# A planned attention and MLP block: prologue over four PSUM banks with keys first, another form of the normalization, an own home for the last group's outputs, contiguous value bursts

## The chip, the cores and the metric

The kernel runs on one core of a Trainium2 chip. The metric is the device time in microseconds (us) of one execution; a kernel's time is the median of its runs. Profiles are taken by the hardware profiler on one execution. The engines are PE (matmuls; PEld is its weight load), DVE (vector), ACT (scalar, with exponential and tanh), POOL (GpSimd) and SP, which issues the DMAs.

## The reference

```
x = A_x                                    # 1 x 2048 x 1024, bf16
xn = layernorm(x)
qkv = xn @ wqkv                            # 32 heads of 32
p = softmax(q k^T * 32**-0.5)
s = (p v, heads joined) @ wo
y = layernorm(xn)                          # the MLP normalizes again
h = gelu(y @ w1 + b1)                      # tanh form, 1024 -> 3584
g = silu(h @ w2 + b2)                      # 3584 -> 1024
out = x + s * g
```

## The kernel before

All work is first written down as a list of operations, each with the tiles it reads and writes, an assumed duration and a priority. A planner (`_Plan.run`) then plays the five engines forward in time with these assumed durations and so fixes the order of instructions on each engine; `settle` derives the semaphore waits from it. On the chip each engine goes through its list in that order and stops where a wait is not yet fulfilled, whatever stands behind it.

**The opening ("pro").** The 2048 tokens are sixteen tiles of 128. For a pair of tiles DVE takes the statistics (L657, L659), POOL raises variance + epsilon to the power -0.5 (L664) and normalizes each tile (L667: subtract the mean, then multiply by the reciprocal deviation) into one of four buffers `xnb`. PE transposes the tile into a PSUM bank (L644), and ACT copies it to `xnT` (L647; the profile names it `big`). From two transposed tiles PE makes queries and keys of the first head group together (one bank, L634 takes both out to `qk`), and values (L617).

**The second normalization.** Its scale per token comes from the first one's variance: four small POOL operations (L679 to L683), the last a power over all sixteen tiles, then a store to DRAM (L684) and a load that spreads 256 tokens' scales over all partitions (`sbc`, L715). Between the two SP also issues the loads of the biases b1 (L685) and b2 (L686). DVE multiplies `xnT` by `sbc` to make `yT` (L718), the MLP's input for 256 tokens.

**Attention.** The 32 heads form eight groups of four. A unit is one group, 256 queries and 256 keys; there are 512. For a unit PE makes scores into four of six PSUM banks (0 to 5; L862), ACT takes two exponentials of 128x1024 into one of nine buffers `P` (L871), DVE adds the two key blocks (`PA`, L874), and PE multiplies with the values and, from `PA` and a tile of ones, the sums of the softmax. Eight units make a group of queries: their value products go into one bank as a burst ("pv"), and DVE divides by the sums (L901 to L907). A burst is opened, in the planner, after the exponential of the sixth unit of its group (`xs[5]`). Outputs of the first seven head groups are stored to DRAM (L950) and reloaded for the last projection (L924); those of the eighth are written straight into `OTr`, which lies where `xnT` was, once nobody reads `xnT` any more (the list `dead`).

**Dense work.** Projections of the next head group ("proj"), the MLP ("mlp": w1, GELU in L738 to L748, w2, L775 to L780) and the output projection ("wo") run in items that fill one PSUM bank each. Together with the value bursts they have banks 6 and 7. All these matmuls are issued by the helper `quad`, so they share the line L544; the tiles' names tell them apart.

In the planner PE takes scores first, then the open burst, then dense chunks, with a pace that holds scores back where dense work lags. The opening's items are taken strictly in the order of their list.

Of the kernel before, what the change touches and what calls it, by code (L numbers as in the profile page):

```python
# [30 lines left out]
class _Plan:  # L31
# [46 lines left out]
    def run(self, total_units, dense_slack):  # L78
# [9 lines left out]
        bank_free = {6: [], 7: []}  # L88
        owner = {6: None, 7: None}
        heads = {q: 0 for q in self.queues}  # L90
        dense_total = sum(c.occ for q in ("proj", "mlp", "wo") for it in self.queues[q] for c in it.chunks)
# [13 lines left out]
        def commit(o, t):  # L105
            e = o.eng
            o.start = t
            if e == "SP":
                tf[e] = t + o.occ
                state["bw"] = max(state["bw"], t) + o.nbytes / 170.0  # L110
                o.fin = state["bw"] + 1900.0
            else:
                tf[e] = t + o.occ
                o.fin = t + o.occ + o.lat
            order[e].append(o)
            self.seq.append(o)
            release(o, t)
            wake(tf[e], e)
# [66 lines left out]
        def pe_step(t):  # L185
            cands = []
            nxt = INF
            if state["s"] < len(self.s_queue):
                o = self.s_queue[state["s"]]
                if o.left == 0:  # L190
                    cands.append((o.ready, 0, o, None))
# [25 lines left out]
            else:  # L217
                bf = bank_for(t)
                if bf is not None:
                    for n in next_items(t):  # L220
                        it = self.queues[n][heads[n]]
# [169 lines left out]
def bass_recurrent_scan__mha_block__mixer_channel_mlp__prompt_kernel(  # L391
# [14 lines left out]
    HG = 8  # L406
# [17 lines left out]
    plan = _Plan()  # L424
    add = plan.add

    with ExitStack() as st:
# [22 lines left out]
        wv = qk0[:, 4096 + 3072:4096 + 3072 + 2048].rearrange("p (c n) -> p c n", c=DC)  # L450
        wo_sb = qk0[:, 0:8192].rearrange("p (c n) -> p c n", c=HG)
# [23 lines left out]
        lnp = sb("lnp", [128, NT, 4], F32)  # L475
# [19 lines left out]
        def c_ps(n):  # L495
            return 133 + 1.04 * n
# [103 lines left out]
        def v_item(pr, n, kind, due=0):  # L600
# [20 lines left out]
        def qk_pair_item(n):  # L621
            it = _Item("pro")
            for k in range(8):
                w, dcs = k // 4, (2 * (k % 4), 2 * (k % 4) + 1)
# [9 lines left out]
            dve(lambda e: e.tensor_copy(QKT[0][:, :, n * 256:(n + 1) * 256],  # L634
                                        bank(it.bank).rearrange("p (w s) -> p w s", w=2)),
                c_ps(512), [], [("Q", 0, n), ("K", 0, n)], 0, it)
# [17 lines left out]
        for n in range(NPR):  # L654
            for t in (2 * n, 2 * n + 1):
                for c in range(2):
# [6 lines left out]
                [("mv", lo), ("mv", lo + 1)], [("ve", n)], 1)  # L663
            pool(lambda e, lo=lo, hi=hi: e.tensor_tensor(lnp[:, lo:hi, 1], lnp[:, lo:hi, 0], mhalf[:, lo:hi], op=ALU.pow),  # L664
                 450, [("ve", n), ("mhalf",)], [("rs", n)], 0)
            for t in (lo, lo + 1):
                pool(lambda e, t=t: e.tensor_scalar(xnb[t % 4], xst[t], mv[:, t, 0:1], lnp[:, t, 1:2],  # L667
                                                    op0=ALU.subtract, op1=ALU.mult), 950,
                     [XS(t), ("mv", t), ("rs", n)], [("xnb", t % 4)], 1)
            its = [tr_item(lo), tr_item(lo + 1), qk_pair_item(n), v_item(0, n, "pro")]  # L670
            if n == 0:
                pro_q += its[0:3]
                late = its[3]
            else:
                pro_q += its[0:3] + [late]
                late = its[3]
        pro_q.append(late)
# [174 lines left out]
        def unit(u, pv):  # L852
# [3 lines left out]
            b0 = [(4 * u + j) % 6 for j in range(4)]  # L856
# [53 lines left out]
        OTr = xnT  # L910
        for w in range(HG):
            if w + 1 < HG:
                proj(w + 1, w)
            else:

                dead = []
                for t in range(NT):
                    for d in [plan.last_w[("xnT", t)]] + plan.readers[("xnT", t)]:
                        if d not in dead:
                            dead.append(d)  # L920
                wdead = [("Q", 0, n) for n in range(NPR)] + [("K", 0, n) for n in range(NPR)] + \
                        [("wqk", i) for i in range(3)] + [("wv",)]
                for hg in range(HG - 1):
                    dma(f"otl{hg}", lambda e, hg=hg: e.dma_start(OTr[:, hg, :], o_d[hg]), 524288,  # L924
                        [("o_d", hg, q) for q in range(NQB)], [("OTr", hg)], extra=dead)
                dma("wo", lambda e: e.dma_start(wo_sb, A_wo.rearrange("(c p) n -> p c n", p=128)), 2097152, [],
                    wdead + [("wo",)])
            for qb in range(NQB):
# [16 lines left out]
                pv.trigger = xs[5] if g < HG * NQB - 1 else xs[0]  # L945
# [7 lines left out]
                norm(g, pv, OTr[:, w, qb * 256:(qb + 1) * 256], [("OTr", w, qb)], dead)  # L953

                for t2 in range(2):
# [18 lines left out]
                    for nh in range(2):  # L974
                        it = _Item("wo")
                        for hc in range(HG):
                            def fn(e, b, hc=hc, tb=tb, nh=nh):
                                return quad(e, lambda j: bankp(b, j, 0, 512),
                                            lambda j: OTr[:, hc, tb * 128 + 32 * j:tb * 128 + 32 * j + 32],
# [72 lines left out]
```

## Time and profile before

| | |
|---|---|
| median of 2 runs | 1227.2 us (1226.93 to 1227.46) |
| profiled execution | 1225.87 us, span 1224.1 us |
| busy, PE / ACT / DVE / POOL | 1069.9 / 1040.2 / 848.6 / 71.2 us |
| exponentials (1024) | 976.5 us of ACT, 1111 ns each |
| HBM traffic | 143.40 MB read, 12.07 MB written |

The profile names a line by L and its number, then the tile written and the tiles read. An engine's idle time is put down to what ended it. PE instructions are pipelined, so a burst's duration divided by its count, not the mean of one, is what a matmul costs.

### The profile page before, as it was taken

The page shows a single profiled execution, that of the slowest core. Times are in us where ns is not written, and L with a number is a line of the kernel's source. Part 1 is how long each engine was busy: PE and PEld are TensorE (multiplying, and loading weights), DVE is VectorE, ACT ScalarE, POOL GpSimd, SP SyncE. Part 2 cuts the span into 40 slices and gives each one's busy share as a digit, 9 for nine tenths or more (in the row PEclk, how much of TensorE's full clock was granted, in tenths as well). Part 3 has the DMA queues.
Part 4 walks back from the last instruction along what each step waited for, and adds up shares of the span by engine and source line. Part 5 has one row for each costly group of instructions (what it writes and reads, how often), then busy time and mean ns, then how long its engine had stood idle before and what let it go on. Part 6 is the DMA issues. An engine that isn't in the chain of part 4 may idle for free.

```text
span 1224.1 us, 63652 instructions
## 1 busy us (share of the span) xinstructions
PE 1069.9 (87%) x30080; PEld 717.9 (59%) x30080; DVE 848.6 (69%) x1531; ACT 1040.2 (85%) x1186; POOL 71.2 (6%) x34
## 2 busy tenths in 40 slices
PE   4636999999999999999999998999989997778998
PEld 2524666756766576656776566656766664456443
DVE  4613897778676886786668866976678776554676
ACT  2414998999899999998999988999999999866894
POOL 6960000000000000000000000000000000000000
PEclk8876999999999999999999999999999998789999
DMA  7032446633365445533365445533355456426242
GB/s 232 2 61 52 121 128 179 179 99 85 109 172 156 137 142 159 162 85 102 108 183 147 126 126 167 169 97 90 103 168 147 134 149 210 142 75 193 83 141 96
DMA packets 289268, 159.55 MB, mean 130 GB/s; under 512 B 28912, under 2 KB 278768, under 8 KB 289008
## 3 DMA queue, kind: packets, MB, share of 16 engines
q1 hardware_dynamic: 289008, 155.49, 44.4%
q8 instruction: 235, 3.85, 1.3%
q14 instruction: 25, 0.20, 0.1%
HBM read 143.40 MB, written 12.07 MB: 127 GB/s over the span
## 4 chain that ended last, share of the span: by engine, by line
PE 49%; ACT 37%; POOL 5%; DVE 5%; issue 3%; SPq 1%; DMA 1%; POOLq 0%; ACTq 0%; DVEq 0%
PE ps L544 41%; ACT P L871 34%; PE ps L862 8%; POOL gw L667 4%; ACT ut L746 2%; SPq L686 1%; DVE PA L874 1%; ACT gw L779 1%; DVE nt L901 1%; DMA sbc<-s_scratch 1%; DVE xb L738 0%; POOL lnp L664 0%; PE ps L644 0%; DVE V L617 0%; DVE ut L744 0%
## 5 line engine op out<-in xcount | busy, mean ns | idle before, releaser
L871 ACT ACTIVATE P<-ps 128x1024 bf16<-128x1024 f32 x1024 | 976.5, 1111 | 136.6 <-PE ps L862 135.9
L874 DVE TENSOR_TENSOR PA<-P 128x1024 bf16<-128x1024 bf16 x512 | 351.7, 688 | 210.1 <-ACT P L871 204.3
L544 PE MATMUL ps<-yT,w1r 128*32 128x256 bf16 x7168 | 238.6, 273 | 12.7 <-DVE QKT L831 3.9
L544 PE MATMUL ps<-w2r,hT 128*32 128x256 bf16 x7168 | 232.3, 273 | 12.0 <-issue 5.2
L544 PEld LDWEIGHTS ps<-yT,w1r 128*32 128x32 bf16 x7168 | 178.5, 96 | 55.4 <-issue 29.5
L544 PEld LDWEIGHTS ps<-w2r,hT 128*32 128x32 bf16 x7168 | 182.4, 97 | 41.7 <-issue 27.4
L544 PE MATMUL ps<-P,V 128*32 128x256 bf16 x4096 | 170.7, 280 | 16.8 <-issue 8.6
L544 PE MATMUL ps<-big,qk 128*32 128x512 bf16 (+1 forms) x2304 | 141.5, 374 | 14.5 <-ACT big L647 8.5
L544 PE MATMUL ps<-qk,big 128*32 128x256 bf16 (+1 forms) x3072 | 137.1, 318 | 6.7 <-DVE gw L775 1.4
L862 PE MATMUL ps<-qk 32*128 32x256 bf16 x2048 | 104.7, 277 | 40.6 <-DVE qk L634 25.2
L544 PEld LDWEIGHTS ps<-P,V 128*32 128x32 bf16 x4096 | 104.9, 98 | 45.1 <-ACT P L871 18.1
L544 PE MATMUL ps<-PA,ones 128*32 128x256 bf16 x2048 | 126.4, 277 | 1.9 <-issue 1.6
L862 PE MATMUL ps<-QKT 32*128 32x256 bf16 x2048 | 103.5, 276 | 23.0 <-ACT P L871 22.1
L544 PEld LDWEIGHTS ps<-qk,big 128*32 128x32 bf16 x3072 | 77.8, 99 | 46.3 <-issue 13.1
L544 PEld LDWEIGHTS ps<-big,qk 128*32 128x32 bf16 x2304 | 57.5, 102 | 63.3 <-issue 15.1
L862 PEld LDWEIGHTS ps<-qk 32*128 32x128 bf16 x2048 | 30.9, 92 | 107.5 <-ACT P L871 65.7
L746 ACT ACTIVATE ut<-ut 128x512 f32<-128x512 f32 x112 | 83.4, 745 | 4.3 <-DVE ut L744 4.1
L738 DVE TENSOR_TENSOR xb<-ps,b1T 128x512 bf16<-128x512 f32 x112 | 76.8, 686 | 14.2 <-PE ps L544 13.7
L748 DVE SCALAR_TENSOR_TENSOR hT<-ut,xb 128x512 bf16<-128x512 f32 x112 | 76.1, 680 | 15.1 <-ACT ut L746 14.7
L862 PEld LDWEIGHTS ps<-QKT 32*128 32x128 bf16 x2048 | 30.7, 92 | 94.4 <-ACT P L871 80.8
L744 DVE SCALAR_TENSOR_TENSOR ut<-sq,xb 128x512 f32<-128x512 bf16 x112 | 76.7, 684 | 1.0
L544 PEld LDWEIGHTS ps<-PA,ones 128*32 128x32 bf16 x2048 | 57.3, 98 | 22.7 <-issue 13.7
(45 smaller groups left out, 466.3 us busy)
## 6 DMA issues: line engine op xcount, KB each, us to landing
w1r<-in_B_w_dram SPq DMA_DIRECT2D x112, 512.0 KB, 4.2
w2r<-in_B_w_dram SPq DMA_DIRECT2D x128, 448.0 KB, 4.4
qk<-in_A_wqkv_dram SPq DMA_DIRECT2D x16, 256.0 KB, 3.1
g_scratch<-gw SPq DMA_DIRECT2D x32, 128.0 KB, 2.9
o_scratch<-ot SPq DMA_DIRECT2D x56, 64.0 KB, 2.8
big<-o_scratch SPq DMA_DIRECT2D x7, 512.0 KB, 6.5
hT<-in_A_x_dram SPq DMA_DIRECT2D x10, 256.0 KB, 7.4
qk<-in_A_wqkv_dram SPq DMA_DIRECT2D x4, 512.0 KB, 4.4
```

The source lines that it names most:

```text
L544: ins = e.matmul(dst(j), lhsT=lhsT(j), rhs=rhs(j), start=start, stop=stop, tile_position=(0, 32 * j), skip_group_check=True)
L667: pool(lambda e, t=t: e.tensor_scalar(xnb[t % 4], xst[t], mv[:, t, 0:1], lnp[:, t, 1:2], op0=ALU.subtract, op1=ALU.mult), 950, [XS(t), ("m ...
L686: dma("b2", lambda e: e.dma_start(b2b[:], B_b2.rearrange("(o d) -> o d", o=1).to_broadcast([128, D])), 262144, [("s3",)], [("b2",)])
L738: dve(lambda e: e.tensor_tensor(xb_t[i3][:].rearrange("p (k t) -> p k t", k=2), bank(it.bank).rearrange("p (k t) -> p k t", k=2), b1T[:, 2 ...
L744: dve(lambda e: e.scalar_tensor_tensor(ut_t[i3][:], sq_t[p % 2][:], 1.0 / GA, xb_t[i3][:], op0=ALU.add, op1=ALU.mult), c_f32(512), [("sq", ...
L746: act(lambda e: e.activation(ut_t[i3][:], ut_t[i3][:], ACT.Tanh, scale=GC * GA), c_act(512), [("ut", i3)], [("ut", i3)], 1)
L748: dve(lambda e: e.scalar_tensor_tensor(hT[:, hs].rearrange("p k t -> p (k t)"), ut_t[i3][:], 1.0, xb_t[i3][:], op0=ALU.add, op1=ALU.mult), ...
L779: act(lambda e: e.activation(zh_t[zi], z_t[zi], ACT.Tanh, scale=0.5), c_act(512), [("z", zi)], [("zh", zi)], 1)
L862: ins = e.matmul(bank(b0[j], kk * 256, (kk + 1) * 256), lhsT=QKT[sl][32 * j:32 * j + 32, 1, kb * 128:(kb + 1) * 128], rhs=QKT[sl][32 * j:3 ...
L871: x = act(lambda e, h=h: e.activation(P[pi][:, 2 * h:2 * h + 2].rearrange("p j k q -> p (j k q)"), ps[:, pr[h] * 1024:(pr[h] + 1) * 1024], ...
L874: pa = dve(lambda e: e.tensor_tensor(PA[ai][:], P[pi][:, :, 0, :], P[pi][:, :, 1, :], op=ALU.add), c_b16(1024), [("P", pi, 0), ("P", pi, 1 ...
L901: a = dve(lambda e: e.transpose(nt_t[i][:], bank(pv.bank, 256, 512)), c_ps(256), [], [("nt", i)], 1, pv)
```

## The change

It has five parts.

1. **Prologue banks and order.** While the opening's transposes, keys and first queries are under way ("due" 0), its items may also use PSUM banks 4 and 5 (`flex`); the first eight units of scores (`NARROW`) stay in banks 0 to 3, and the ninth waits until 4 and 5 are free. Keys are made for every pair of tiles, but queries only for the first two pairs' tokens: those of pair 0 with its keys, those of pair 1 as an item of its own. Queries of the other tokens become three 512-wide items of "proj". Values follow two pairs behind. Of the next eight opening items the planner now takes one that is ready.
2. **Normalization.** POOL now multiplies by the reciprocal deviation and adds a bias, `x * r + (-mean * r)`. The negated mean is one more small DVE operation a pair, its product with r one more small POOL operation a pair.
3. **Last group's outputs** go into `ot7`, a piece of `qk0` behind `wo_sb`, and wait only for the readers of the value weights that lay there.
4. **Value bursts** open after the eighth exponential (`TRIG` = 7).
5. **The planner's assumptions**: DVE's reads of PSUM shorter by 63 ns, DMA at 210 in place of 170 bytes a nanosecond, the small power at 700 in place of 450 ns, and DVE does not begin an operation of low priority shortly before one of high priority falls due.

```
-        bank_free = {6: [], 7: []}
+        bank_free = {b: [] for b in (4, 5, 6, 7)}
+        flex = [6, 7, 4, 5]
...
-                state["bw"] = max(state["bw"], t) + o.nbytes / 170.0
+                state["bw"] = max(state["bw"], t) + o.nbytes / 210.0
...
+            if best is not None and e == "DVE" and best.prio >= 2 and soon[e]:
+                r = min((x[0] for x in soon[e] if x[2].prio <= 1), default=INF)
+                if r < t + best.occ - 400:
+                    wake(r, e)
+                    return None
...
-            for b in (6, 7):
+            for b in flex:
...
+                if state["s"] == self.narrow:
+                    if len(flex) == 2 and o.left == 0 and all(owner[b] is None or owner[b].k == len(owner[b].chunks) for b in (4, 5)):
...
+                        if n == "pro":
+                            q = self.queues["pro"]
+                            best = None
+                            for k in range(heads["pro"], min(len(q), heads["pro"] + 8)):
...
+                            if best[1].due == 0:
+                                state["early"] -= 1
+                                if state["early"] == 0:
+                                    del flex[2:]
+                            q.insert(heads["pro"], q.pop(k))
...
+        ot7 = qk0[:, 8192:10240]
...
-            return 133 + 1.04 * n
+            return 70 + 1.04 * n
...
+        def k_pair_item(n, with_q):
+            return pair_item(n, (1, 0) if with_q else (1,))
+        def q_pair_item(n):
+            return pair_item(n, (0,))
...
+            dve(lambda e, lo=lo, hi=hi: e.tensor_scalar_mul(lnp[:, lo:hi, 4], mv[:, lo:hi, 0], -1.0), 65,
+                [("mv", lo), ("mv", lo + 1)], [("nm", n)], 1)
...
+            pool(lambda e, lo=lo, hi=hi: e.tensor_tensor(lnp[:, lo:hi, 5], lnp[:, lo:hi, 4], lnp[:, lo:hi, 1], op=ALU.mult),
+                 200, [("nm", n), ("rs", n)], [("nb_", n)], 0)
             for t in (lo, lo + 1):
-                pool(lambda e, t=t: e.tensor_scalar(xnb[t % 4], xst[t], mv[:, t, 0:1], lnp[:, t, 1:2],
-                                                    op0=ALU.subtract, op1=ALU.mult), 950,
+                pool(lambda e, t=t: e.tensor_scalar(xnb[t % 4], xst[t], lnp[:, t, 1:2], lnp[:, t, 5:6],
+                                                    op0=ALU.mult, op1=ALU.add), 950,
...
+            pro_q += [tr_item(lo), tr_item(lo + 1), k_pair_item(n, n == 0)]
+            if n >= 2:
+                pro_q.append(v_item(0, n - 2, "pro"))
+        pro_q.append(q_pair_item(1))
+        pro_q.append(v_item(0, 6, "pro"))
+        pro_q.append(v_item(0, 7, "pro"))
...
-            b0 = [(4 * u + j) % 6 for j in range(4)]
+            k0 = 0 if u < NARROW else 2 * (u - NARROW) + 2
+            b0 = [(2 * k0 + j) % 6 for j in range(4)]
...
+        for tq in range(1, 4):
+            plan.queues["proj"].append(qk_item(0, 0, tq, wq0, 16 * tq - 12))
...
-                pv.trigger = xs[5] if g < HG * NQB - 1 else xs[0]
+                pv.trigger = xs[TRIG] if g < HG * NQB - 1 else xs[0]
...
-                norm(g, pv, OTr[:, w, qb * 256:(qb + 1) * 256], [("OTr", w, qb)], dead)
+                norm(g, pv, ot7[:, qb * 256:(qb + 1) * 256], [("OTr", w, qb)], dead7)
```

Some lines of the last output projection follow from `ot7` and are not shown.

More of the change, by code (lines that the diff above doesn't have):

```diff
@@ L87, in run @@
                  "done": 0.0, "last_bank": 7}
-        bank_free = {6: [], 7: []}
-        owner = {6: None, 7: None}
+        bank_free = {b: [] for b in (4, 5, 6, 7)}
+        owner = {b: None for b in (4, 5, 6, 7)}
+        flex = [6, 7, 4, 5]
         heads = {q: 0 for q in self.queues}
+        state["early"] = sum(it.due == 0 for it in self.queues["pro"])
         dense_total = sum(c.occ for q in ("proj", "mlp", "wo") for it in self.queues[q] for c in it.chunks)
@@ L189, in pe_step @@
                 o = self.s_queue[state["s"]]
-                if o.left == 0:
+                if state["s"] == self.narrow:
+                    if len(flex) == 2 and o.left == 0 and all(owner[b] is None or owner[b].k == len(owner[b].chunks) for b in (4, 5)):
+                        xs = bank_free[4] + bank_free[5]
+                        if all(x.start is not None for x in xs):
+                            cands.append((max([o.ready] + [x.fin for x in xs]), 0, o, None))
+                            for x in xs:
+                                o.deps[x] = True
+                elif o.left == 0:
                     cands.append((o.ready, 0, o, None))
@@ L920, in bass_recurrent_scan__mha_block__mixer_channel_mlp__prompt_kernel @@
                             dead.append(d)
-                wdead = [("Q", 0, n) for n in range(NPR)] + [("K", 0, n) for n in range(NPR)] + \
+                wdead_ = [("Q", 0, n) for n in range(NPR)] + [("K", 0, n) for n in range(NPR)] + \
                         [("wqk", i) for i in range(3)] + [("wv",)]
+                dead7 = [d for d in [plan.last_w[("wv",)]] + plan.readers[("wv",)]]
                 for hg in range(HG - 1):
```

48 lines of the change are left out of this document (29 added, 19 removed).

## The prediction

> **What bounds it now.** I read the page first, then busy time by stretches, then the opening in order of time, then the waits. The page gives the span, each engine's share, and the span in 40 slices of 30.6 us.
>
> ```profile
> span 1224.1 us, 63652 instructions
> PE 1069.9 (87%) x30080; PEld 717.9 (59%) x30080; DVE 848.6 (69%) x1531; ACT 1040.2 (85%) x1186; POOL 71.2 (6%) x34
> PE   4636999999999999999999998999989997778998
> POOL 6960000000000000000000000000000000000000
> ```
>
> PE and ACT are both near full for most of the run, so neither alone is the bound. Two stretches fall short: the first four slices, the only ones in which POOL works, and slices 33 to 36. The stretches show it (columns: window, length, then busy us of PE, PEld, DVE, ACT, POOL, granted clock, DMA share, GB/s):
>
> ```profile
> 72.00:80.00 8.00, 1.31 (x48) 1.01 (x40) 0.00 (x0) 0.00 (x0) 8.00 (x3) 0.87 0.17 12
> 80.00:90.00 10.00, 0.00 (x0) 0.00 (x0) 0.00 (x0) 0.00 (x0) 1.95 (x1) 0.50 0.40 34
> 400.00:500.00 100.00, 93.45 (x2748) 63.76 (x2748) 77.60 (x141) 97.39 (x113) 0.00 (x0) 1.00 0.53 148
> 1000.00:1050.00 50.00, 38.44 (x1032) 24.50 (x1028) 31.68 (x55) 45.44 (x53) 0.00 (x0) 0.86 0.56 171
> 1050.00:1100.00 50.00, 36.01 (x924) 23.72 (x920) 29.24 (x53) 36.16 (x41) 0.00 (x0) 0.83 0.36 113
> ```
>
> The opening in order of time (start, length, engine, line, tiles; in brackets the idle time before and what ended it):
>
> ```profile
> 36.45 7.54 POOL L667 TENSOR_SCALAR gw<-hT,mv,lnp 128x1024 bf16<-128x1024 bf16 x2
> 44.78 7.54 POOL L667 TENSOR_SCALAR gw<-hT,mv,lnp 128x1024 bf16<-128x1024 bf16 x2
> 71.47 2.94 POOL L683 TENSOR_TENSOR lnp<-lnp,mhalf 128x16 f32<-128x16 f32 x1
> 74.40 7.55 POOL L667 TENSOR_SCALAR gw<-w2r,mv,lnp 128x1024 bf16<-128x1024 bf16 x2
> 74.44 0.37 SPq L684 DMA_DIRECT2D s_scratch<-lnp  x1
> 75.84 11.06 SPq L686 DMA_DIRECT2D b2b<-in_B_b_dram  x1
> 88.02 9.81 SPq L715 DMA_DIRECT2D sbc<-s_scratch  x2
> 94.37 1.90 DVE L718 TENSOR_TENSOR yT<-big,sbc 128x512 bf16<-128x512 bf16 x3 [24.57 <-DMA sbc<-s_scratch]
> 96.92 0.61 PE L862 MATMUL ps<-qk 32*128 32x256 bf16 x8 [23.62 <-DVE qk L634]
> 97.47 3.60 PE L544 MATMUL ps<-qk,big 128*32 128x256 bf16 x64
> 124.05 0.62 PE L544 MATMUL ps<-yT,w1r 128*32 128x256 bf16 x16 [0.77 <-DVE QKT L831]
> ```
>
> Up to 82 us the opening goes at POOL's pace, 8.33 us a pair of tiles. Then the second norm's scale goes through DRAM: its power ends at 74.41, DVE gets it at 94.37, and what is queued behind DVE's wait keeps PE still for 23.6 us. The MLP starts at 124.05. From there on both engines are near full (93.45 and 97.39 of 100), so what is saved before it moves the end by as much.
>
> **The normalization's price.** One tile costs 7.54 / 2 = 3.77 us. Rows for bounds:
>
> ```profile
> 0.24 0.10 POOL L1037 MEMSET const-float32-0.0<- 128x1 f32 x1 [0.24 <-issue]
> 0.82 0.24 POOL L587 IOTA iota_i<- 128x128 int32 x1 [0.39 <-POOLq L1037]
> 6.65 0.71 POOL L664 TENSOR_TENSOR lnp<-lnp,mhalf 128x2 f32<-128x2 f32 x1 [5.05 <-DVE lnp L662]
> 70.45 0.24 POOL L679 TENSOR_TENSOR lnp<-mv,lnp 128x16 f32<-128x16 f32 x1
> 71.09 0.30 POOL L682 TENSOR_SCALAR lnp<-lnp 128x16 f32<-128x16 f32 x1
> ```
>
> High end: 3.77, the same tile in the old form. Low end: the IOTA writes 127 elements a partition more than the MEMSET in 0.14 us, 1.1 ns each; 1024 of them and 0.10 make 1.2 us. The old form's 3.7 ns an element is no limit of moving data, and not contention: from 74.40 it takes 7.55 a pair while DVE is idle. On POOL the operation sets the price: the power takes (2.94 - 0.71) / 14 = 0.16 us an element, while 16 multiplies or 16 adds fit in 0.24 to 0.30. The new form multiplies, then adds. I take 1.2, with 3.77 as the first rival.
>
> The Trainium skill (GPSIMD Engine Reference, Engine selection) has one-input operations on this engine at about line rate; at its 1.2 GHz that is an estimate of 0.9 us, and the sum would be 1 us lower. The old form at 3.77 does not agree, so the page cannot tell the two forms apart. Its Key points speak against the change: POOL shares an interface with VectorE. By that the faster form could slow down beside DVE's statistics; the 7.54 and 7.55 with DVE busy and idle show none of it for the old form.
>
> **The opening, step by step.** On POOL the second scale now stands last:
>
> ```order
> L713 TENSOR_TENSOR lnp<-lnp,mhalf 128x2
> L718 TENSOR_SCALAR gw<-w2r,lnp 128x1024
> L715 TENSOR_TENSOR lnp<-lnp 128x2
> L728 TENSOR_TENSOR lnp<-mv,lnp 128x16
> L718 TENSOR_SCALAR gw<-w2r,lnp 128x1024 x2
> L730 TENSOR_TENSOR lnp<-lnp 128x16
> L731 TENSOR_SCALAR lnp<-lnp 128x16
> L732 TENSOR_TENSOR lnp<-lnp,mhalf 128x16
> ```
>
> Before, the power (L683) stood ahead of the last two tiles. On DVE, where yT waits for that scale, before:
>
> ```order
> L874 TENSOR_TENSOR PA<-P 128x1024
> L718 TENSOR_TENSOR yT<-big,sbc 128x512 x3
> L634 CAST qk<-ps 128x2x256
> L718 TENSOR_TENSOR yT<-big,sbc 128x512
> L617 CAST V<-ps 128x2x2x128
> ```
>
> and now:
>
> ```order
> L653 CAST V<-ps 128x2x2x128
> L924 TENSOR_TENSOR PA<-P 128x1024
> L682 CAST qk<-ps 128x256
> L767 TENSOR_TENSOR yT<-big,sbc 128x512 x3
> L653 CAST V<-ps 128x2x2x128
> L767 TENSOR_TENSOR yT<-big,sbc 128x512
> L924 TENSOR_TENSOR PA<-P 128x1024 x2
> L653 CAST V<-ps 128x2x2x128
> ```
>
> All keys are now out of PSUM ahead of yT; two value casts and the first group's value product are left behind it (before, also the last two transposes and the last two key pairs). So PE still stops for sbc, but less waits behind it. Prices for DVE and PE:
>
> ```profile
> 10.67 0.61 DVE L662 TENSOR_SCALAR lnp<-mv 128x2 f32<-128x2 f32 x1
> 17.22 3.24 PE L544 MATMUL ps<-big,qk 128*32 128x256 bf16 x64 [1.11 <-ACT big L647]
> 20.52 0.69 DVE L634 CAST qk<-ps 128x512 bf16<-128x512 f32 x1 [9.24 <-PE ps L544]
> 22.44 0.21 DVE L659 BATCH_NORM_AGGREGATE mv<-stats 128x2 f32<-128x12 f32 x1
> 23.83 0.21 DVE L659 BATCH_NORM_AGGREGATE mv<-stats 128x2 f32<-128x12 f32 x1
> 71.39 1.92 PE L544 MATMUL ps<-big,qk 128*32 128x256 bf16 x64
> 121.06 1.90 PE L544 MATMUL ps<-big,qk 128*32 128x512 bf16 x32
> 123.92 0.41 DVE L907 TENSOR_TENSOR ot<-ps,nb 128x256 bf16<-128x256 f32 x1
> ```
>
> With POOL at about 3.6 us a pair (two tiles at 1.2, 0.71, 0.24, gaps) the statistics on DVE set the pace. They stand at 11.3 us after two pairs. To come: twelve tiles at 1.39 (22.44 to 23.83), 16.7; twelve small scalars at 0.15, 1.8, the added negated mean among them; ahead of the last scalars five wide casts at 0.69 and three 256-wide ones, nearest row L907 at 0.41, 4.7. One wait is sure: the first keys cannot leave PSUM before about 16 (tiles normalized at 10.2, transposes, copies and 3.24 of cold matmuls), DVE is there at 12.6: 3.4. That makes 37.9; for further waits on a PE that starts cold I add 4 (0 to 14: at 3.24 / 64 the 544 matmuls and twelve transposes ahead of the last such cast last to 52). So 42. POOL then needs 0.71 + 3 x 1.2 + 2 x 0.24 + 0.23 + 0.30 + 2.94 and gaps, 9 in all: the power ends at 51. The way through DRAM took 94.37 - 74.41 = 20.0; SP still issues the slow b2 load between store and return, but the two w2 loads that stood ahead of sbc are now issued before the store: 18, with 17 and 21 as ends. yT at 69. Behind it: three yT 1.9, a cast 0.7, then on PE some 96 matmuls of the first group and the last values at the cold 0.05, two scores, a cast and one 512-wide query item at 1.9: 11. **The MLP starts at 80 in place of 124: 44 gained**, 34 to 52.
>
> Given back: query items 1 to 3 leave the opening. In the order, 96 more 512-wide matmuls stand in all and 32 fewer are done by then, 128 x 1.9 / 32 = 7.6, and one score unit less is done, 0.6: **8.2 lost**.
>
> **The last groups.** In the 32 score units from 432 on, PE's order before holds 596 dense matmuls of 256 columns (a 512-wide one as two), now 1264. Before:
>
> ```order
> L544 MATMUL ps<-yT,w1r 32x256 x8
> L544 MATMUL ps<-P,V 32x256 x8
> L544 MATMUL ps<-PA,ones 32x256 x16
> L862 MATMUL ps<-qk 128x256 x48
> L544 MATMUL ps<-P,V 32x256 x32
> ```
>
> and now, at the same place:
>
> ```order
> L580 MATMUL ps<-PA,ones 32x256 x16
> L912 MATMUL ps<-qk 128x256 x24
> L580 MATMUL ps<-yT,w1r 32x256 x32
> L912 MATMUL ps<-qk 128x256 x8
> L580 MATMUL ps<-yT,w1r 32x256 x48
> L912 MATMUL ps<-qk 128x256 x8
> ```
>
> Six units in a row left PE nothing to do but wait for ACT. From 1000 to 1100 PE is busy 74.5; at the 93.5% of 400 to 500 that takes 79.7: 20 us lost. Holding 668 matmuls more, 20 us at 1.92 / 64, the stretch fills most of it; runs of three units are left. **12 gained**, 0 to 20. The new home of the last outputs (ot7) I cost at nothing: before, no wait for the old home shows in this stage.
>
> **Value bursts and the rest.** The burst now opens after the group's eighth exponential, not the sixth, and holds its bank for less time. From 130 to 990 us:
>
> ```profile
> ACT P L871 <- PE ps L862: 40.9, 44, 4.5
> PE ps L544 <- DVE xb L738: 5.5, 12, 0.7
> PE ps L544 <- DVE gw L775: 3.9, 8, 0.6
> ```
>
> Evictions that hold PE are worth 9.4, so that is the gain's end here; against it eight of nine P buffers are full when the burst opens, at 0.2 for each of 63 openings 13 lost. I take 0.
>
> **Sum.** 1224.1 - 44 + 8.2 - 12 = 1176.3 span. The profiled execution took 1225.87, 1.8 more than its span, and 1.3 less than the median 1227.2: **1179**.
>
> **Rivals.**
> *The form does not matter* (3.77 stays). For it: the only row of this tile. A pair then takes 8.33 + 0.3, with one wait of 4 for DVE as now: tiles done at 80, power at 84, yT at 103, MLP at 114; 10 - 8.2 + 12 gained: **1213**. Chance 0.18.
> *PE stays cold through the opening.* For it: clock 0.50 to 0.87 after each idle stretch, 3.24 for 64 matmuls against 1.92. The statistics end at 52, ten later: **1189**. Against: PE has less idle time between items now. Chance 0.12.
> *The bursts starve ACT.* With one P buffer left, an exponential waits until the burst has freed the first; PE may be in the middle of other work then. Nearest rows:
>
> ```profile
> 319.12 5.61 ACT L871 ACTIVATE P<-ps 128x1024 bf16<-128x1024 f32 x6 [0.57 <-PE ps L862]
> ```
>
> At 0.57 for each of 63 openings 36 is lost; from 48 / 63 = 0.76 on the kernel is slower than before; at 1.2 it takes 1179 + 76 = **1255**, slower. Against: the ninth buffer covers 5.61 / 6 x 2 = 1.9 us, and a burst frees its first buffer within eight matmuls. Chance 0.08, half of it above 2%.
>
> **How the numbers follow.** Forecast 0.62; its own range is 1152 to 1200 (MLP start, the last groups, bursts). With the first rival 1150 to 1215 leaves out 2 in 10. Two per cent, about what a measurement of this kernel tells from no change, is 24.5 us: faster means below 1202.7. The forecast gives 0.59 of that, the cold opening 0.10, the first rival 0.03: 0.73 with the rest. Slower 0.05, within 0.22.
>
> **What would show it.** In the new line numbers, right: POOL's L718 near 1.2 a tile, its L732 ending near 51, yT near 69, the first yT matmul near 80; PE above 80 busy from 1000 on in each 100 until the last scores; no new idle time of ACT ahead of each ninth exponential. Wrong: tiles at 3.77; a matmul of w1 later than 100; ACT waiting for PE much above 41 in the middle.

## The result, and the profile after

The changed kernel takes **1148.1 us** (median of 2 runs, 1144.6 to 1151.7), where the kernel before takes 1227.2: a ratio of 0.936, with a 95% interval of 0.923 to 0.948. In four further runs it took 1149.1, a ratio of 0.938 (0.934 to 0.942). The forecast was 1179 with 1150 as the low end: the right direction, a gain some 31 us too small, and a time just below the range.

The page of the changed kernel:

```profile
PE 1046.8 (92%) x29984; PEld 714.6 (63%) x29984; DVE 853.4 (75%) x1543; ACT 1039.5 (91%) x1186; POOL 32.7 (3%) x42
PE   5769999999989999999999899999999998789997
POOL 5600000000000000000000000000000000000000
```

The span is 1140.5 us. POOL is at work in two slices and no longer in three, and the dip near the end is shallower (8, 7 and 8 tenths, where PE had 7, 7, 7 and 8). The same stretches as before (window, length, busy us of PE, PEld, DVE, ACT, POOL, granted clock, DMA share, GB/s):

```profile
72.00:80.00 8.00, 7.76 (x228) 5.56 (x232) 6.51 (x14) 5.66 (x7) 0.00 (x0) 1.00 0.48 135
80.00:90.00 10.00, 9.92 (x284) 6.56 (x274) 9.41 (x18) 10.00 (x13) 0.00 (x0) 1.00 0.60 167
400.00:500.00 100.00, 95.79 (x2768) 64.74 (x2757) 78.02 (x140) 98.08 (x115) 0.00 (x0) 1.00 0.50 141
1000.00:1050.00 50.00, 44.66 (x1360) 32.65 (x1364) 27.52 (x48) 42.33 (x50) 0.00 (x0) 1.00 0.57 173
1050.00:1100.00 50.00, 49.13 (x1080) 23.72 (x1076) 39.17 (x74) 49.03 (x54) 0.00 (x0) 1.00 0.39 121
```

From 72 to 90 us, where PE had 1.31 us of work and POOL was still normalizing, PE is now full. The opening in order of time:

```profile
35.80 1.20 POOL L718 TENSOR_SCALAR gw<-w2r,lnp 128x1024 bf16<-128x1024 bf16 x1
36.92 0.15 DVE L711 TENSOR_SCALAR lnp<-mv 128x2 f32<-128x2 f32 x1
44.42 2.95 POOL L732 TENSOR_TENSOR lnp<-lnp,mhalf 128x16 f32<-128x16 f32 x1
47.40 0.37 SPq L733 DMA_DIRECT2D s_scratch<-lnp  x1
50.24 9.36 SPq L735 DMA_DIRECT2D b2b<-in_B_b_dram  x1
63.44 1.90 DVE L767 TENSOR_TENSOR yT<-big,sbc 128x512 bf16<-128x512 bf16 x3 [13.48 <-DMA sbc<-s_scratch]
65.99 1.90 PE L580 MATMUL ps<-P,V 128*32 128x256 bf16 x32 [7.78 <-DVE V L653]
75.07 1.93 PE L580 MATMUL ps<-yT,w1r 128*32 128x256 bf16 x64
```

A tile costs 1.20 us. DVE still stops for the scales (13.48 us), and PE behind it for the value cast (7.78 us, where before it stood 23.62). The MLP starts at 75.07 where it started at 124.05: 49.0 us earlier. The waits from 130 to 990 us (total, times, longest):

```profile
ACT P L921 <- PE ps L912: 22.9, 40, 2.6
ACT P L921 <- PE ps L580: 7.5, 12, 1.9
PE ps L580 <- DVE xb L787: 5.3, 12, 0.6
PE ps L580 <- DVE gw L824: 0.9, 2, 0.5
```

ACT's wait for scores fell from 40.9 to 22.9. The second row is new: here ACT waits for the helper `quad` (L580, before L544), that is for a value burst that still reads the buffer `P` which the next exponential is to fill. These two rows decide the case.

**Where the time came from.** The 1024 exponentials are the same in every kernel here, so their progress divides the run into the same stages. A boundary is the end of the named exponential (line L871, now L921) in the trace; the last stage ends with the span. The expectations below speak of 12 us for the middle and of 20 to 22 for the last groups, from coarser readings of the same stages.

| stage, us | before | changed | changed, once more |
|---|---|---|---|
| to the 26th exponential (opening) | 125.3 | 79.3 | 81.4 |
| 26th to 896th (middle) | 923.6 | 909.4 | 913.0 |
| 896th to 960th (last groups) | 93.1 | 74.6 | 76.7 |
| 960th to the end | 82.1 | 77.2 | 77.2 |
| span | 1224.1 | 1140.5 | 1148.4 |

The opening gave 46.0, the middle 14.2, the last groups 18.5, the end 4.9. The prediction had 44 for the opening, 8.2 *lost* behind it, and 12 for the last groups. In the middle ACT is busy for 873 us before and for 875 in both profiles of the changed kernel; the rest is its idle time, 50.7 us before, 34.5 and 38.0 now.

### The profile page after: what moved, and what is told of

Read it like the earlier page. It is cut to its first block, busy times and chain, and to the rows that moved or that the text cites. A ratio compares the mean times of both kernels' runs of the same rounds, so it can differ in the third digit from the quotient of the medians.

```text
span 1140.5 us, 63544 instructions
## 1 busy us (share of the span) xinstructions
PE 1046.8 (92%) x29984; PEld 714.6 (63%) x29984; DVE 853.4 (75%) x1543; ACT 1039.5 (91%) x1186; POOL 32.7 (3%) x42
## 4 chain that ended last, share of the span: by engine, by line
PE 63%; ACT 27%; DVE 4%; issue 3%; SPq 1%; POOL 1%; DMA 1%; POOLq 0%; ACTq 0%
PE ps L580 53%; ACT P L921 25%; PE ps L912 10%; ACT ut L795 2%; DVE stats L704 1%; SPq L735 1%; DVE xb L787 1%; DVE nt L951 1%; POOL gw L718 0%; ACT gw L828 0%; DMA sbc<-s_scratch 0%; DVE V L653 0%; POOLq L1057 0%; DMA hT<-in_A_x_dram 0%; SPq L734 0%
## 5 line engine op out<-in xcount | busy, mean ns | idle before, releaser
L921 ACT ACTIVATE P<-ps 128x1024 bf16<-128x1024 f32 x1024 | 970.4, 1087 | 69.4 <-PE ps L912 47.0
L580 PE MATMUL ps<-yT,w1r 128*32 128x256 bf16 x7168 | 235.9, 274 | 10.2 <-issue 6.7
L580 PE MATMUL ps<-w2r,hT 128*32 128x256 bf16 x7168 | 230.3, 273 | 8.6 <-issue 5.4
L580 PEld LDWEIGHTS ps<-yT,w1r 128*32 128x32 bf16 x7168 | 179.5, 97 | 52.9 <-issue 35.5
L580 PEld LDWEIGHTS ps<-w2r,hT 128*32 128x32 bf16 x7168 | 181.2, 97 | 41.7 <-issue 32.4
L580 PE MATMUL ps<-P,V 128*32 128x256 bf16 x4096 | 161.6, 276 | 12.1 <-DVE V L653 8.6
L580 PE MATMUL ps<-big,qk 128*32 128x512 bf16 (+1 forms) x2208 | 133.7, 369 | 5.4 <-DVE xb L787 3.1
L580 PE MATMUL ps<-qk,big 128*32 128x256 bf16 (+1 forms) x2944 | 126.4, 307 | 6.2 <-ACT big L694 2.0
L580 PEld LDWEIGHTS ps<-P,V 128*32 128x32 bf16 x4096 | 109.5, 98 | 28.0 <-DVE V L653 9.3
L912 PE MATMUL ps<-qk 32*128 32x256 bf16 x2048 | 105.0, 275 | 21.8 <-ACT P L921 14.8
L580 PE MATMUL ps<-PA,ones 128*32 128x256 bf16 x2048 | 120.7, 275 | 3.2 <-issue 3.0
L912 PE MATMUL ps<-QKT 32*128 32x256 bf16 x2048 | 102.7, 273 | 11.5 <-ACT P L921 9.8
L580 PEld LDWEIGHTS ps<-qk,big 128*32 128x32 bf16 x2944 | 72.6, 97 | 40.9 <-issue 14.3
L787 DVE TENSOR_TENSOR xb<-ps,b1T 128x512 bf16<-128x512 f32 x112 | 76.8, 686 | 18.7 <-PE ps L580 17.7
L580 PEld LDWEIGHTS ps<-big,qk 128*32 128x32 bf16 x2208 | 53.8, 97 | 53.4 <-issue 13.7
L912 PEld LDWEIGHTS ps<-qk 32*128 32x128 bf16 x2048 | 31.3, 92 | 87.8 <-ACT P L921 58.6
L912 PEld LDWEIGHTS ps<-QKT 32*128 32x128 bf16 x2048 | 30.7, 92 | 81.1 <-ACT P L921 67.2
L795 ACT ACTIVATE ut<-ut 128x512 f32<-128x512 f32 x112 | 77.8, 698 | 2.8 <-DVE ut L793 2.8
L793 DVE SCALAR_TENSOR_TENSOR ut<-sq,xb 128x512 f32<-128x512 bf16 x112 | 76.7, 686 | 1.7
L580 PEld LDWEIGHTS ps<-PA,ones 128*32 128x32 bf16 x2048 | 55.6, 97 | 19.3 <-issue 16.9
```

Of the source, the lines that this page charges most:

```text
L580: ins = e.matmul(dst(j), lhsT=lhsT(j), rhs=rhs(j), start=start, stop=stop, tile_position=(0, 32 * j), skip_group_check=True)
L787: dve(lambda e: e.tensor_tensor(xb_t[i3][:].rearrange("p (k t) -> p k t", k=2), bank(it.bank).rearrange("p (k t) -> p k t", k=2), b1T[:, 2 ...
L793: dve(lambda e: e.scalar_tensor_tensor(ut_t[i3][:], sq_t[p % 2][:], 1.0 / GA, xb_t[i3][:], op0=ALU.add, op1=ALU.mult), c_f32(512), [("sq", ...
L795: act(lambda e: e.activation(ut_t[i3][:], ut_t[i3][:], ACT.Tanh, scale=GC * GA), c_act(512), [("ut", i3)], [("ut", i3)], 1)
L912: ins = e.matmul(bank(b0[j], kk * 256, (kk + 1) * 256), lhsT=QKT[sl][32 * j:32 * j + 32, 1, kb * 128:(kb + 1) * 128], rhs=QKT[sl][32 * j:3 ...
L921: x = act(lambda e, h=h: e.activation(P[pi][:, 2 * h:2 * h + 2].rearrange("p j k q -> p (j k q)"), ps[:, pr[h] * 1024:(pr[h] + 1) * 1024], ...
```

## The experiments

Each kernel is compared with the kernel before on the same chip (1225.2 to 1227.0 there). Where two edited kernels are compared, the difference of their ratios is taken times 1226 us.

### The opening: the form and the order, each alone

The kernel before with the new form, its order of items unchanged:

```
-  e.tensor_scalar(xnb[t % 4], xst[t], mv[:, t, 0:1], lnp[:, t, 1:2], op0=ALU.subtract, op1=ALU.mult)
+  e.tensor_scalar(xnb[t % 4], xst[t], lnp[:, t, 1:2], lnp[:, t, 5:6], op0=ALU.mult, op1=ALU.add)
```

with the two small operations that make the bias.

> The kernel before with the multiply-add form alone; the plan's order of everything else stays. Theory A (the form alone makes the opening fast; DVE's statistics then set the pace): POOL tiles 1.2 us each, first yT matmul near 88 in place of 124 (yT near 66, and the last two key pairs, three value casts and a softmax division still behind it: about 20), so about 1191. Rival (the four banks and keys first are needed to use it): POOL waits for free tiles, first yT matmul not before 110, 1213 or more.

Measured: 1199.4 us, ratio 0.977 (0.975 to 0.980). Order of time in its opening:

```profile
36.73 2.37 POOL L671 TENSOR_SCALAR gw<-w2r,lnp 128x1024 bf16<-128x1024 bf16 x2
51.59 2.80 POOL L671 TENSOR_SCALAR gw<-w2r,lnp 128x1024 bf16<-128x1024 bf16 x2 [0.83 <-PE ps L644]
70.60 2.50 DVE L722 TENSOR_TENSOR yT<-big,sbc 128x512 bf16<-128x512 bf16 x4 [2.09 <-DMA sbc<-s_scratch]
97.85 0.62 PE L544 MATMUL ps<-yT,w1r 128*32 128x256 bf16 x16 [0.74 <-DVE QKT L835]
```

The tiles cost 1.2 here too, so the price belongs to the form. But POOL now waits for PE to take the tiles, and the MLP starts 27 us behind yT: as before, the last two transposes, two pairs of keys and queries (128 matmuls) and three items of values (192) still stand between. The time lies between the two theories.

The changed kernel with the old form, everything else kept:

```
-  e.tensor_scalar(xnb[t % 4], xst[t], lnp[:, t, 1:2], lnp[:, t, 5:6], op0=ALU.mult, op1=ALU.add)
+  e.tensor_scalar(xnb[t % 4], xst[t], mv[:, t, 0:1], lnp[:, t, 1:2], op0=ALU.subtract, op1=ALU.mult)
```

> The changed kernel with subtract-multiply back on POOL, the order of all instructions unchanged. Theory A: tiles 3.77 again, tiles done at 80, first yT matmul near 114, so 39 later than the 75 measured: about 1187. Rival (the bank and order change carries part of the opening's gain): first yT matmul before 100, under 1172.

Measured: 1185.5, ratio 0.967 (0.963 to 0.970).

```profile
70.02 7.54 POOL L718 TENSOR_SCALAR gw<-w2r,mv,lnp 128x1024 bf16<-128x1024 bf16 x2
97.52 1.89 DVE L767 TENSOR_TENSOR yT<-big,sbc 128x512 bf16<-128x512 bf16 x3 [13.04 <-DMA sbc<-s_scratch]
109.13 1.93 PE L580 MATMUL ps<-yT,w1r 128*32 128x256 bf16 x64
```

The MLP starts 11.6 us behind yT (109.13 - 97.52), as in the changed kernel (75.07 - 63.44). So the form alone starts the MLP 26.2 us earlier, the order alone 14.9, both 49.0: together 7.9 more than the sum. With the old form the order waits for POOL's tiles; with the new form alone the work that stands behind yT is in the way.

### The last groups: the planner's DMA rate and the outputs' home

The kernel before, planned with 210 bytes a nanosecond instead of 170; then the changed kernel with 170:

```
-  state["bw"] = max(state["bw"], t) + o.nbytes / 170.0
+  state["bw"] = max(state["bw"], t) + o.nbytes / 210.0
```

> The kernel before, planned with DMA at 210 in place of 170 bytes a nanosecond, nothing else. In units 416 to 447 its PE order holds 1160 dense matmuls in place of 1032. Theory B (the assumed DMA speed starved the plan's last groups): the 20 us that the last 80 units give go with it, 1207, and the time between exponentials 928 and 960 falls from 54 to about 35. Rival (it is the other home, the burst trigger or DVE's holding back): 1227 within 5.

> The changed kernel, planned with DMA at 170 again. Theory B: the last groups lose about 20, so about 1168. Rival: 1148 within 5.

Measured: 1213.7, ratio 0.989 (0.987 to 0.991); and 1169.9, ratio 0.954 (0.951 to 0.956). One row each of the busy time by stretches, 896th to 960th exponential, first the kernel before, then the changed one, then the changed one with 170:

```profile
1048.90:1142.00 93.10, 72.35 (x1996) 49.48 (x1996) 47.50 (x83) 65.38 (x74) 0.00 (x0) 0.91 0.46 139
```

```profile
988.70:1063.20 74.50, 67.70 (x1952) 46.24 (x1948) 47.62 (x84) 64.08 (x74) 0.00 (x0) 1.00 0.54 169
```

```profile
988.40:1087.10 98.70, 76.48 (x2080) 53.45 (x2076) 50.01 (x87) 64.00 (x74) 0.00 (x0) 0.89 0.45 139
```

With 170 the stall is back in full, 98.7 us against 93.1, and the granted clock falls with it. In the kernel before, 210 shortens this stage from 93.1 to 77.7 but lengthens the middle by 5.7, so its time lies between the two theories.

The last outputs in their old home; PE's order does not change:

```
-  norm(g, pv, ot7[:, qb * 256:(qb + 1) * 256], [("OTr", w, qb)], dead7)
+  norm(g, pv, OTr[:, w, qb * 256:(qb + 1) * 256], [("OTr", w, qb)], dead)
```

> The changed kernel with the last group's outputs in the old home; PE's order is the same, only DVE's waits differ. Prediction (nothing waits there on the chip): 1148 within 4. Rival (the old home's wait holds the last bursts): some of the last groups' 22 us come back, 1155 or more.

Measured: 1155.2, ratio 0.940 (0.936 to 0.945); its interval overlaps that of the changed kernel, but the time lies outside the 1148 within 4 that was expected and at the foot of the rival's range. Its middle (916.9) lies among those of three other runs with this order of PE (909.4 to 917.4). Its last groups took 80.0 us against 74.6 to 76.7 there, at a granted clock of 0.94 against 0.98 to 1.00, and no wait of DVE for the old home stands in that stage. So no row shows a cost of the home, but these runs do not rule out a few us.

### The middle: three of the planner's numbers undone, one at a time

```
-    TRIG = 7
+    TRIG = 5
```

> The changed kernel with bursts opened after the sixth exponential again. Theory C (contiguous bursts give the 12 us gained between exponentials 26 and 896): about 1160, and PE's waits for evictions from 130 to 990 rise. Theory D (bursts are neutral, as predicted; the gain comes from other parts of the plan): 1148 within 5.

```
-            if best is not None and e == "DVE" and best.prio >= 2 and soon[e]:
+            if False:
```

> The changed kernel without DVE's holding back of low-priority operations. Theory E (evictions that come sooner give the middle's 12 us): about 1158. If neutral: 1148 within 5.

```
-            return 70 + 1.04 * n
+            return 133 + 1.04 * n
```

> The changed kernel, planned with DVE's reads of PSUM 63 ns longer again. If the plan's truer eviction time gives the middle's gain: about 1158; if neutral: 1148 within 5.

Measured: 1174.1, ratio 0.957 (0.953 to 0.960), for early bursts; 1161.6, ratio 0.946 (0.944 to 0.948), without the holding back; 1165.0, ratio 0.950 (0.946 to 0.953), with the longer PSUM reads. All three lose, and nearly all of it in the middle (935.9, 926.5 and 931.6 us against 909.4 and 913.0). Before each is given a price of its own, one must know what any re-planning costs. So two numbers were moved that no engine could notice:

```
-  state["bw"] = max(state["bw"], t) + o.nbytes / 210.0
+  state["bw"] = max(state["bw"], t) + o.nbytes / 215.0
```

```
-  e.tensor_scalar_mul(lnp[:, lo:hi, 4], mv[:, lo:hi, 0], -1.0), 65,
+  e.tensor_scalar_mul(lnp[:, lo:hi, 4], mv[:, lo:hi, 0], -1.0), 75,
```

> The changed kernel again, unedited, as the ground for its three neighbours on this chip. One profile and the timed runs before gave 1144.6 to 1151.7; the kernel with the last outputs back in their old home, whose TensorE order is the same, gave 1149 to 1159. If the time of this one plan is steady, 1144 to 1152; if it wanders by itself by ten us, 1144 to 1160, and then a loss of 13 us by an edit says less.

> Only the planner's DMA rate moves, from 210 to 215 B/ns; no instruction is added, removed or changed, only their order. Theory A (each part of the planner's new numbers has its own worth, so a neighbouring plan is as good): 1144 to 1154. Theory B (the changed kernel's plan is a favourable one among neighbours that lie 10 to 25 us above it, and any edit of a number loses that): 1158 to 1172, with the loss between the 128th and the 896th exponential.

> Only the planned time of the instruction that negates the means moves, from 65 to 75 ns, which no engine could notice; the order of the later instructions shifts with it. Theory A (parts have their own worth): 1144 to 1154. Theory B (a favourable plan): 1158 to 1172, lost in the middle as with the other neighbours.

Measured: 1149.1 (ratio 0.938) for the changed kernel itself, 1153.5 (0.941; 0.937 to 0.945) with 215, 1161.9 (0.949; 0.945 to 0.952) with 75. Neither theory holds cleanly: one neighbour lost 4 us, the other 13. The changed kernel's plan is the best of the three, and a loss of up to 13 us says nothing of the number that was edited. By that the holding back (9.7 us) and the PSUM reads (14) cannot be told from a mere re-planning; the bursts (23) lie above it.

### Early bursts in other plans

Late bursts against early ones were therefore repeated: in the two neighbouring plans, and in the kernel before, there also with the shorter reads. The neighbours have `TRIG = 5` as above; in the kernel before the index itself is edited:

```
-                pv.trigger = xs[5] if g < HG * NQB - 1 else xs[0]
+                pv.trigger = xs[7] if g < HG * NQB - 1 else xs[0]
```

> The changed kernel with the bursts opened after the sixth exponential again, in the plan that comes with the negated mean at 75 ns. Its neighbour with late bursts took 1161.9 and its ACT waited 32.6 us for scores from 130 to 990. Theory A (late bursts are worth about 25 us by themselves, because ACT then waits less for scores): 1180 to 1190, and a wait of 45 to 55. Theory B (each plan falls as it falls, and the loss of 26 belonged to that one plan): 1155 to 1170, a wait of 25 to 40.

> The same pair of numbers in the plan that comes with 215 B/ns; the neighbour with late bursts took 1153.5 and waited 27.6 us for scores. Theory A: 1172 to 1182, a wait of 45 to 55. Theory B: 1148 to 1165, a wait of 23 to 40.

> The kernel before with its bursts opened after the eighth exponential, nothing else. In the kernel before, ACT waited 40.9 us for scores from 130 to 990. Theory A (late bursts are worth it in any plan): the wait falls to about 25, the time by 15 to 25, to 1202 to 1212. Theory C (late bursts pay only with the planner's shorter PSUM reads, which decide when a bank comes free): 1220 to 1230.

> The kernel before with late bursts and with DVE's reads of PSUM planned 63 ns shorter. Theory A: 1200 to 1212, the shorter reads adding 0 to 5. Theory C: the two together give 15 to 25 where the bursts alone give nothing. If neither the bursts nor the reads move it (1220 to 1230), the middle's gain needs the changed opening as well.

Measured: 1170.5, ratio 0.955 (0.952 to 0.957); 1171.9, ratio 0.956 (0.953 to 0.958); 1203.2, ratio 0.981 (0.979 to 0.984); 1200.1, ratio 0.980 (0.976 to 0.984). The table has the four pairs. ACT's waits are those for scores (L912, L862) and for the burst (L580, L544) from 130 to 990 us; the middle is the stage from the 26th to the 896th exponential; a long stretch is a place in PE's order where more than 120 matmuls (a 512-wide one as two, transposes left out) stand between one score unit and the next, from the 16th unit to the 430th.

| plan: early, late bursts | gain of late bursts, us | ACT's wait for scores | ACT's wait for the burst | middle | ACT idle in the middle | long stretches |
|---|---|---|---|---|---|---|
| changed | 23 | 48.6, 23.6 | 0.4, 10.3 | 935.9, 913.0 | 60.5, 38.0 | 7, 1 |
| 215 B/ns | 18 | 48.3, 27.6 | 0.4, 7.0 | 936.4, 920.2 | 61.8, 44.1 | 7, 2 |
| mean at 75 ns | 7 | 46.0, 32.6 | 0.4, 6.9 | 930.2, 924.6 | 54.2, 48.4 | 6, 5 |
| before | 23 | 40.9, 27.4 | 0, 8.0 | 923.6, 913.2 | 50.7, 40.2 | 8, 5 |

The rows of the first pair in the view of the waits (changed kernel with early bursts, then its second profile with late ones):

```profile
ACT P L921 <- PE ps L912: 48.6, 53, 4.3
ACT P L921 <- PE ps L580: 0.4, 1, 0.4
```

```profile
ACT P L921 <- PE ps L912: 23.6, 42, 2.3
ACT P L921 <- PE ps L580: 10.3, 15, 1.9
```

Late bursts gain in all four, 7 to 23 us, though the 7 lies within the 13 us between neighbouring plans. (That plan with early bursts took a time of Theory B and a wait of Theory A.) ACT waits 13 to 25 us less for scores and 7 to 10 us more for the burst. What is left of the two is seen in its idle time: ACT is busy for 873 to 876 us of the middle in all eight kernels, and the middle shortens by 22.9, 16.2, 5.6 and 10.4 us where ACT's idle time falls by 22.5, 17.7, 5.8 and 10.5. One pair is not independent: apart from the opening and one place near the end, PE's order with early bursts is the same with 215 as with 210. Those two kernels repeat one plan on two chips (1174.1 and 1171.9). In the kernel before, the 25.4 us by which the span fell lie in the opening (6.3), the middle (10.4), the last groups (7.8) and the end (1.0): there the later bursts re-planned the other stages too. The shorter reads add 2 us to it, inside the intervals.

What such a wait looks like in the kernel before, PE alone in order of time, and ACT's row at its end:

```profile
562.97 0.40 PE L862 MATMUL ps<-QKT 32*128 32x256 bf16 x8
563.30 2.48 PE L544 MATMUL ps<-w2r,hT 128*32 128x256 bf16 x84
...
567.24 2.57 PE L544 MATMUL ps<-w2r,hT 128*32 128x256 bf16 x88
569.74 0.40 PE L862 MATMUL ps<-QKT 32*128 32x256 bf16 x8
```

```profile
570.19 1.02 ACT L871 ACTIVATE P<-ps 128x1024 bf16<-128x1024 f32 x1 [4.53 <-PE ps L862]
```

PE isn't idle for one moment here. Between two score units, 6.4 us apart, stand 172 matmuls of w2 and, at the dots, 60 of a burst (48 with the values, 12 for the sums), and ACT, with 1.9 us of exponentials to a unit, runs dry for 4.53. Why the planner puts dense work and an early burst in one stretch was not traced; that there are fewer such stretches with late bursts is the table's last column.

The wait for the burst, in the changed kernel: PE's rows, then ACT's.

```profile
440.67 0.84 PE L580 MATMUL ps<-P,V 128*32 128x256 bf16 x24
441.33 0.28 PE L580 MATMUL ps<-PA,ones 128*32 128x256 bf16 x4
```

```profile
441.67 1.02 ACT L921 ACTIVATE P<-ps 128x1024 bf16<-128x1024 f32 x1 [0.94 <-PE ps L580]
```

With the eight at 440.00, 32 value matmuls stand ahead of the first four for the sums, and with these the exponential is released: in the program a buffer `P` counts as read only when the matmuls for the sums of its unit are done too.

### The way of the scales through DRAM

The loads of b1 and b2 issued behind the x loads, no longer between the store and the load of the scales:

```
-  ..., 8192, [("s3",)], [("b1",)])
+  ..., 8192, [], [("b1",)])
...
-            [("s3",)], [("b2",)])
+            [], [("b2",)])
```

> The loads of the two bias vectors are issued right behind the x loads, and no longer between the store and the load of the scales; TensorE's order is unchanged. Theory A (the wait for the scales is SyncE's: b2's issue held the queue from 50.24 to 59.60): the load of the scales is issued at about 50 to 51, the first yT multiplication starts near 54 to 55 where it started at 63.4, and the time falls by 5 to 9 us, to about 1140. Theory B (the store itself lands only about 11 us after its issue, at 59): the load of the scales waits for it all the same, the first yT multiplication stays at 62 to 63, and the time is that of the changed kernel within 3 us.

Measured: 1150.9 (1145.2 to 1152.7), ratio 0.939 (0.934 to 0.943): no gain. In order of time, then the wait of SP's queue:

```profile
47.65 0.37 SPq L733 DMA_DIRECT2D s_scratch<-lnp  x1
58.86 0.34 SPq L764 DMA_DIRECT2D sbc<-s_scratch  x1
62.07 1.89 DVE L767 TENSOR_TENSOR yT<-big,sbc 128x512 bf16<-128x512 bf16 x3 [11.86 <-DMA sbc<-s_scratch]
```

```profile
SPq L764 <- DMA s_scratch<-lnp: 10.8, 1, 10.8
```

Theory B holds. With nothing to issue, SP waits 10.8 us for the store itself, which lands 11.2 us after its issue began (58.86 - 47.65). No kernel tried here is faster than the changed one.

## Why the prediction was right in its direction and short in its size

**The price on POOL: right.** 1.2 us a tile was taken, 1.20 measured, and 3.77 comes back with the old form. The rival that the form does not matter is gone; the share of the two halves of the opening is shown by the two undone kernels.

**The opening: right, a little pessimistic.** DVE's last scalars came at 37 and not at 42, the power ended at 47.4 and not at 51, yT stood at 63.4 and not at 69, the MLP started at 75 and not at 80. The 4 us added for a cold PE were not needed: the first pair's 64 matmuls still took 3.28, but from the second pair on they took 1.9 to 2.0.

```profile
20.54 1.98 PE L580 MATMUL ps<-qk,big 128*32 128x256 bf16 x64 [1.63 <-ACT big L694]
```

The rival of a cold PE falls with that row. The way through DRAM took 16.1 against the 18 assumed, and for another reason than the one given: b2's issue did stand between store and load, but the store takes about as long by itself. 49.0 us were gained where 44 were forecast.

**The term that failed: the value bursts.** "Evictions that hold PE are worth 9.4, so that is the gain's end here ... I take 0." The step that failed is this bound. The two rows of evictions hardly move with the bursts: together they stand at 6.4 us with early bursts in the changed kernel (3.5 and 2.9) and at 6.2 with late ones (5.3 and 0.9). The row above that sentence read 40.9 us of ACT waiting for scores, and the prediction used it only as a limit for what might get worse. It was what the bursts change: with late ones ACT waits 13 to 25 us less for scores, and by its idle time the middle of the changed kernel is 22.9 us shorter. The bound of the gain was taken from the wait that the edit touches directly (a bank held longer) and not from the wait of the other engine that is full, which sees every matmul that stands ahead of its scores.

The rival that late bursts starve ACT was right in kind: its wait appears, 7.5 and 10.3 us in 12 and 15 places of the two profiles against 0.4 with early bursts, so the sign "no new idle time of ACT" was not met. It was priced for each of 63 openings, and what is saved on scores is more. The reason given against it, a first buffer freed within eight matmuls, does not hold: the rows above show 32 and four more.

With that one term undone the rest of the sum can be read. The changed kernel with early bursts has a span of 1170.3; its stages against the kernel before, beside the terms as forecast:

| term, us | forecast | early bursts against before |
|---|---|---|
| opening | -44 | -47.9 |
| given back, middle | +8.2 | +12.3 |
| last groups and end | -12 | -14.0 - 4.2 |
| late bursts | 0 | not in this kernel |
| span | 1176.3 | 1170.3 |

The middle's 12.3 lost agrees with the 8.2 given back, but also holds whatever the other new numbers of the planner do; by the 13 us of scatter between plans that can't be separated. The late bursts then take the span to 1140.5 and 1148.4 in the two profiles of the changed kernel, 23 to 27 us of it in the middle.

**The last groups: right in place, somewhat small.** The stage gained 16.4 to 18.5 where 12 were taken and 20 was the end of the range; about 2 to 5 of it goes with the late bursts (79.1 us with early ones, 74.6 and 76.7 with late ones). The prediction read the cure from the order and named no cause. The DMA rate is enough to bring the stall back in the changed kernel and to cure most of it in the one before. Yet late bursts alone, at 170, also shorten the stage, to 85.3: the stall belongs to a plan, not to one number.

**What stays open.** Whether the old home costs anything; whether the holding back of DVE and the shorter PSUM reads are worth anything by themselves; by how much the queries moved out of the opening cost; and why the planner strings dense work and bursts together.

## What to carry to other kernels

Where two engines are both near full, the bound on what an edit of the order can gain is the *other* full engine's wait, not the wait at the thing edited: here 40.9 us in one row, of which one changed index took 13.5 in the kernel before. The same index opened a second wait of 8 us on that engine, so what counts in the end is its idle time in the stage, with all its reasons. Where a planner makes the order, an edit of any of its numbers makes a new plan, so time one or two innocuous neighbours first; what lies within their scatter (here 13 us) is no finding, and an effect is believed when it returns in several plans. In an opening, a faster engine pays in full only if the work queued behind its result is moved as well (26 and 15 us apart, 49 together).

## What the runs showed of the hardware that was not expected

**Two forms of one operation, three times the price.** Subtract-then-multiply takes 3.77 us for 128x1024 on POOL, multiply-then-add 1.20, both bf16 with two per-partition scalars, in the same place of the same program.

**POOL and DVE do slow each other, but not for every operation.** POOL's rows of the changed kernel, then DVE's beside them:

```profile
25.09 2.37 POOL L718 TENSOR_SCALAR gw<-hT,lnp 128x1024 bf16<-128x1024 bf16 x2
33.39 1.19 POOL L718 TENSOR_SCALAR gw<-w2r,lnp 128x1024 bf16<-128x1024 bf16 x1
38.22 1.98 POOL L718 TENSOR_SCALAR gw<-w2r,lnp 128x1024 bf16<-128x1024 bf16 x1
40.96 2.80 POOL L718 TENSOR_SCALAR gw<-w2r,lnp 128x1024 bf16<-128x1024 bf16 x2
```

```profile
26.44 1.04 DVE L709 TENSOR_SCALAR lnp<-mv 128x2 f32<-128x2 f32 x1
33.61 0.64 DVE L704 BATCH_NORM_STATS2 stats<-w2r 128x6 f32<-128x512 bf16 x1
37.93 1.27 DVE L924 TENSOR_TENSOR PA<-P 128x1024 bf16<-128x1024 bf16 x2
39.73 1.00 DVE L924 TENSOR_TENSOR PA<-P 128x1024 bf16<-128x1024 bf16 x1
41.32 1.36 DVE L924 TENSOR_TENSOR PA<-P 128x1024 bf16<-128x1024 bf16 x1 [0.25 <-ACT P L921]
46.22 0.68 DVE L924 TENSOR_TENSOR PA<-P 128x1024 bf16<-128x1024 bf16 x1
```

Beside the statistics a tile takes 1.19 and one of the statistics 0.64. Beside the additions of two P halves a tile takes 1.98, two take 2.80, and two of the additions take 1.00 and 1.36 where one takes 0.68 at 46.22. The small operation L709 has one input; it takes 0.15 at 30.91, with POOL idle, but 1.04 at 26.44, where it ends with POOL's two tiles (27.48 and 27.46). The Trainium skill (GPSIMD Engine Reference, Key points) says that POOL shares its interfaces to SBUF with VectorE, with contention with VectorE's instructions in a 2-port performance mode or with two SBUF inputs. The additions agree with the second kind, and the statistics, with one input, were not slowed; whether L709 runs in such a mode no row shows. The prediction drew its worry from the statistics, which have one input, and did not look at the additions. By these rows three tiles on POOL took about 1.2 us longer than at 1.20 each; what that cost the opening no run measured by itself.

**A small store can be slow.** The scales are 8 KB, and their store took 11.3 us to land in the changed kernel and 11.2 with no load of the biases issued behind it, while the loads that spread them landed in 3.3. The transfers issued from 30 to 70 us in the changed kernel, KB each and us from issue to landing:

```profile
s_scratch<-lnp SPq DMA_DIRECT2D x1, 8.0 KB, 11.3
sbc<-s_scratch SPq DMA_DIRECT2D x2, 128.0 KB, 3.3
```

Before, the 11.06 us of b2's issue hid this; they looked like the cause.
